# One list of all engines' work from the first instruction to the end of the second stage, with due times worked back from the products

## The chip, the cores and the metric

The kernel runs on one core of a Trainium2 chip. The metric is the device time of one launch in microseconds (us). In this text PE is TensorE, DVE is VectorE, ACT is ScalarE, POOL is GpSimd and SP is SyncE, whose queue issues the DMAs.

## The reference

Three stages follow each other on 4 sequences of 768 tokens (3072 tokens in all). All arithmetic on the chip is float32; the weights arrive as 64-bit floats.

```
# 1 retention, 8 heads of 64, per sequence b and head h
state = gamma[h] * state + outer(k[t], v[t])
x[t]  = q[t] @ state / 8
# 2 expert layer, 512 -> 2048 -> 512
h = x @ w_in
g = where(h >= 1, h, where(h <= -1, 0, (h + 1)**2 / 4))
x2 = g @ w_out
# 3 expert layer, 512 -> 1024 -> 512
h2 = x2 @ w2_in
u  = h2 * softmax(h2)
out = ((u - mean) / sqrt(var + 1e-6) * g_ln) @ w2_out
```

## The kernel before

**Precision.** A product takes each operand as a rounded part and a remainder (hi, lo) and adds hi·hi, lo·hi and hi·lo, so each product of the layers is three matmuls. Each 128x512 matmul streams 512 columns.

**Weights.** A weight piece (128 rows of 512 numbers) comes as 64-bit words. `conv_w` (L259 to L283) makes float32 words of them: ACT L264 and L267, DVE L265, L268, L269, L270; then the hi part on ACT (L275) and the lo part on DVE (L276). w_in and w_out have 16 pieces each. For pieces from `KEEP` = 4 on, `conv_w` also stores the float32 words to DRAM (`wim`, `wom`, L281).

**Blocks.** The tokens are 6 blocks of 512; four attention units of 128 tokens fill one block, so there are 24 units. A unit is scores (16 small matmuls), a mask on DVE (`sm`), the part that comes from the running state (8 matmuls, or 16 quarter-size ones from unit 12 on), the part within the unit (16), and the new state (16). A sequence has 6 units; its first unit reads no state and its last makes none.

**First stretch, the direct form.** Blocks 0 and 1 go through the first expert layer directly, in 32 slots of one weight piece each: `moe_h` (L529, 12 matmuls), activation on ACT and DVE (L535 to L537, L243, L244), `moe_out` (L557, 12 matmuls). `weights_slot` loads and converts pieces some slots ahead. Units 0 to 15 run beside it, in `attention`. `prep` makes the left operands of the second form from the weights of a pair of pieces: it takes the float32 words (from DRAM through `back`, or for the first `KEEP` pieces as hi + lo, L595), forms four sums (L602), splits them (L243, L244 on 128x1024) and stores seven left operands per pair to DRAM (`wia`, `woa`, L611 and L613): three copies of 256 KB and two stores of 512 KB. The order of this whole stretch is made by the framework's scheduler from the order of the code and its priorities.

**Second stretch, the seven-product form.** Blocks 2 and 3, then 4 and 5, go through the same layer with seven products in place of eight (a Strassen scheme). A first gemm has 8 x 7 products of six matmuls (L947), a second gemm 7 x 8 (L1095). Their left operands are read back from DRAM by `stream` (L700), 256 KB each, four to a buffer. Units 16 to 23 run inside the first of the four gemms (L747 scores, L785, L791, L797). The order comes from the class `Plan`: each task has an engine, a cost, predecessors, a due time given by hand and buffers that it takes; `run` lists them in simulated time, earliest possible first, PE in the order of the code. All five engines then run in that order (`in_row`).

**Third stage.** Loops in the order of the code; PE L1285, L1326 and L1337.

**Buffers.** Most tiles of 4 KB per partition come from one pool "w" with `NWS` = 27 buffers. A unit's q and k tile `qk` has 2 buffers; the result of a unit from 16 on is written into that tile and stored from there (`xrd`, L814), so that the tile comes free when that store has landed.

Of the kernel before, what the change touches and what calls it, by code (L numbers as in the profile page):

```python
# [38 lines left out]
KEEP = 4  # L39
KVACT = 8  # L40
PREP = 12
NWS, NOPS = 27, 6
# [25 lines left out]
class Slot:  # L68


    def __init__(self, pool):
        self.pool, self.users, self.left, self.end = pool, [], 0, None
# [6 lines left out]
class Task:  # L79
    def __init__(self, eng, cost, fn, deps, due, take):  # L80
        self.eng, self.cost, self.fn, self.due, self.take = eng, cost, fn, due, take
        self.deps = [d for d in deps if d is not None]
        self.start = self.end = self.gate = None


class Plan:
# [3 lines left out]
    WAIT = 0.15  # L90

    def __init__(self, caps):
        self.tasks, self.caps, self.clock, self.products, self.lead = [], caps, 0.0, [], 1

    def add(self, eng, cost, fn, deps=(), due=0.0, take=()):
        t = Task(eng, cost, fn, deps, due, take)
        if eng != "PE" and len(self.products) >= self.lead:
            t.gate = self.products[-self.lead]
        self.tasks.append(t)
        return t  # L100

    def ahead(self, lead):

        self.lead = lead

    def pe(self, cost, fn, deps=(), take=()):
        t = self.add("PE", cost, fn, deps, self.clock, take)
# [5 lines left out]
    def run(self):  # L113
        todo, after, slots = {}, {}, {p: [] for p in self.caps}
        ready = {e: [] for e in ("PE", "DVE", "ACT", "POOL", "SP")}
        order = [t for t in self.tasks if t.eng == "PE"][::-1]
        for t in self.tasks:
            before = t.deps + ([t.gate] if t.gate else [])
            todo[t] = len(before)
            for d in before:  # L120
                after.setdefault(d, []).append(t)
            if not before:
                ready[t.eng].append(t)
        uses = {}
        for t in self.tasks:
            for s in t.take:
                s.left = len(s.users)
                for u in s.users:
                    uses.setdefault(u, []).append(s)
        free, dma, left = dict.fromkeys(ready, 0.0), 0.0, len(self.tasks)  # L130

        def can(t):

            at = max([free[t.eng]] + [d.end + Plan.WAIT for d in t.deps] + ([t.gate.start] if t.gate else []))
            for p in {s.pool for s in t.take}:
                n = sum(s.pool == p for s in t.take)
                ends = sorted(9e9 if s.end is None else s.end for s in slots[p])
                over = len(ends) + n - self.caps[p]
                if over > 0:
                    at = max(at, ends[over - 1] + Plan.WAIT)  # L140
            return at

        while left:
            best = None
            for e, ts in ready.items():
                if e == "PE":
                    ts = [t for t in ts if t is order[-1]]
                for t in ts:
                    at = can(t)
                    k = (at if at > free[e] else free[e], t.due)  # L150
                    if at < 9e8 and (best is None or k < best[0]):
                        best = k, t
            if best is None:
                raise RuntimeError(f"the plan is stuck: {[(t.eng, t.due, [s.pool for s in t.take]) for ts in ready.values() for t in ts if t.eng != 'PE' or t is order[-1]]}")
            (at, _), t = best
            ready[t.eng].remove(t)
            if t.eng == "PE":
                order.pop()
            t.start = at
            free[t.eng] = at + (0.34 if t.eng == "SP" else t.cost)  # L160
            if t.eng == "SP":
                dma = max(dma, at + 1.6) + t.cost
                t.end = dma + 0.6
            else:
                t.end = at + t.cost
            for s in t.take:
                slots[s.pool] = [x for x in slots[s.pool] if x.end is None or x.end + Plan.WAIT > at] + [s]
            for s in uses.get(t, ()):
                s.left -= 1
                if not s.left:  # L170
                    s.end = max(u.end for u in s.users)
            t.fn()
            left -= 1
            for u in after.get(t, ()):
                todo[u] -= 1
                if not todo[u]:
                    ready[u.eng].append(u)
        return max(t.end for t in self.tasks if t.eng == "PE")
# [3 lines left out]
def kernel(  # L182
# [64 lines left out]
    wi, wo = {}, {}  # L247
    state = {}

    def load_w(src, pool=wp):  # L250
        raw = pool.tile([128, 512, 2], U32, tag="w", name="w_raw")
        state["last_w"] = nc.sync.dma_start(raw.rearrange("p a t -> p (a t)"), src.bitcast(U32))
        return raw
# [3 lines left out]

    def conv_w(raw, scale=None, w=None, keep=None):
        lw, hw = raw[:, :, 0], raw[:, :, 1]  # L259
        m = cv.tile([128, 512], F32, tag="wm", name="wm", bufs=3)  # L260
        p = cv.tile([128, 512], F32, tag="wp", name="wp", bufs=2)
        mu, mi = m.bitcast(U32), m.bitcast(I32)

        sc.activation(m, hw.bitcast(F32), AF.Abs)  # L264
        ve.tensor_scalar(m, m, W_MIN, W_MAX, op0=ALU.max, op1=ALU.min)  # L265

        sc.activation(p, lw, AF.Copy, bias=2.0, scale=2.0 ** -51)  # L267
        ve.tensor_scalar(mu, mu, 3, None, op0=ALU.logical_shift_left)  # L268
        ve.scalar_tensor_tensor(mu, hw, 0x80000000, mu, op0=ALU.bitwise_and, op1=ALU.bitwise_xor)  # L269
        ve.tensor_tensor(out=mi, in0=mi, in1=p.bitcast(I32), op=ALU.add)  # L270
        if w is None:
            w = wp.tile([128, 2, 512], F32R, tag="w", name="w")
        hi, lo = w[:, 0, :], w[:, 1, :]
        if scale is None:
            sc.activation(hi, m, AF.Copy)  # L275
            ve.tensor_tensor(out=lo, in0=m, in1=fl(hi), op=ALU.subtract)  # L276
        else:
            sc.activation(hi, m, AF.Copy, scale=scale)
            ve.scalar_tensor_tensor(lo, m, scale, fl(hi), op0=ALU.mult, op1=ALU.subtract)
        if keep is not None:  # L280
            nc.sync.dma_start(keep, m)  # L281
        return w

# [18 lines left out]
    def attention(u, env):  # L302
        b, c = divmod(u, NCH)
        first, last = c == 0, c == NCH - 1
        blk, cb = divmod(u, CPB)
        attp = env["attp"]
        if blk == 0:
            def banks(*names):
                return [ps_acc.tile([128, 512], F32, tag="acc", name=n) for n in names]
        else:  # L310
            both = []

            def banks(*names):

                if not both:
                    both.append(ps_a.tile([128, 2, 512], F32, tag="pa", name="pa"))
                return [both[0][:, n] for n in range(len(names))]
        early, quad = u < NWP, u >= QUAD

        def tile_of(name, *shape):  # L320
            if early:
                return wp.tile([128, 2, *shape], F32, tag="w", name=name)
            return attp.tile([128, 2, *shape], F32, tag=name, name=name, bufs=2)

        qk, kv = tile_of("qk", NPAIR, C), tile_of("kv", H, D)
        with (ExitStack() if early else tc.issue_after(state["last_w"].ins)):
            if not quad:
                nc.sync.dma_start(qk, qk_t[b, c])
            else:
                load_swapped(qk, qk_t[b, c])  # L330
            nc.sync.dma_start(kv, kv_t[b, c])
        yield
        yield
        if u == QUAD:

            env["gdec"] = gdec2
            with tc.issue_after(state["last_w"].ins):
                load_swapped(qdec, xtab_d)
                load_swapped(gdec2, gdec_d)
            gp.tensor_tensor(out=qdec, in0=qdec, in1=gdec2.to_broadcast([128, NPAIR, C]), op=ALU.mult)  # L340
            swap = wp.tile([128, 2, 2, C], F32, tag="w", name="swap")
            for r in range(2):
                sc.activation(swap[:, r], dmat[:, r, 2:], AF.Copy)
            for r in range(2):
                sc.activation(dmat[:, r, 2:], swap[:, 1 - r], AF.Copy)
        qp = [t.rearrange("a (p c) -> a p c", p=NPAIR) for t in banks("qp0", "qp1")]
# [1072 lines left out]
```

## Time and profile before

| | us |
|---|---|
| median of 3 runs | 913.42 (911.47 to 914.26) |
| the profiled execution | 916.41 |
| its span, first to last instruction | 914.7 |
| PE busy / weight loads busy | 877.1 / 715.1 |
| DVE busy / ACT busy | 751.1 / 507.0 |
| mean granted PE clock | 0.981 of full speed |

A busy PE is one with a matmul in flight, by modelled ends; it says nothing of the rate. The rate is read from the distance between starts. A granted clock of 1.0 is the higher of two levels (2.4 GHz), 0.5 the lower (1.2 GHz).

### The profile page before, as it was taken

The numbers are of one execution on the slowest core, as the hardware profiler recorded it, in microseconds if no ns is written. First come the engines' busy times: TensorE is split into PE (matmuls) and PEld (weight loads), VectorE is DVE, ScalarE is ACT, GpSimd is POOL, SyncE is SP. The second block draws the span as 40 slices with busy tenths as digits, with TensorE's granted clock in tenths as the row PEclk, the third lists the DMA queues.
The fourth block names the chain that finished last, engine by engine and source line by source line (L and its number), as shares of the span: only waits on it lengthen the run. The fifth ranks groups of instructions, "written<-read, shape, count | busy, mean of one in ns | idle before, by whom it ended". The sixth has DMA issues, their size and how long they took to land. (4 is left out here: it accounts for less than half of the span.)

```text
span 914.7 us, 13934 instructions
## 1 busy us (share of the span) xinstructions
PE 877.1 (96%) x4824; PEld 715.1 (78%) x4824; DVE 751.1 (82%) x1592; ACT 507.0 (55%) x995; POOL 60.0 (7%) x56
## 2 busy tenths in 40 slices
PE   7899899969999999999989999999999999999998
PEld 7777688848887777788868778888888888888886
DVE  4998898888956767697988989796988888888885
ACT  2767875867756779764537877542333333233322
POOL 3100000000000101000111110017000000000000
PEclk8999999979999999899999999999999999999999
DMA  9849968999997998796668887887110110100000
GB/s 337 343 162 339 344 233 271 383 346 369 338 296 239 313 286 289 240 381 231 224 184 294 317 316 231 294 298 253 58 69 25 45 49 28 65 24 24 24 24 34
DMA packets 108567, 197.08 MB, mean 215 GB/s; under 512 B 10193, under 2 KB 49489, under 8 KB 107729
## 3 DMA queue, kind: packets, MB, share of 16 engines
q1 hardware_dynamic: 108496, 196.20, 62.4%
q8 instruction: 38, 0.62, 0.3%
q14 instruction: 33, 0.26, 0.1%
HBM read 135.34 MB, written 60.82 MB: 214 GB/s over the span
## 5 line engine op out<-in xcount | busy, mean ns | idle before, releaser
L1095 PE MATMUL yp<-go,left 128*128 128x512 f32 x672 | 153.9, 390 | 1.9 <-DVE go L1061 1.7
L1095 PEld LDWEIGHTS yp<-go,left 128*128 128x128 f32 x672 | 125.9, 188 | 29.2 <-DVE go L1061 3.1
L947 PE MATMUL hp<-xoh,left 128*128 128x512 f32 x448 | 126.1, 404 | 5.5 <-DVE cs L1144 2.3
L947 PEld LDWEIGHTS hp<-xoh,left 128*128 128x128 f32 x448 | 83.5, 192 | 28.9 <-DVE gl L996 3.2
L1057 ACT ACTIVATE go<-g 128x512 fp32r<-128x512 f32 x112 | 69.3, 629 | 58.7 <-PE yp L1095 28.3
L1285 PE MATMUL h2p<-w,x2h 128*128 128x512 f32 x384 | 97.1, 395 | 0.0
L1337 PE MATMUL op<-w,lh 128*128 128x512 f32 x384 | 91.4, 390 | 0.2 <-ACT lh L243 0.2
L1061 DVE TENSOR_TENSOR go<-g,go 128x512 fp32r<-128x512 f32 x112 | 77.1, 702 | 11.9 <-ACT go L1057 11.0
L1337 PEld LDWEIGHTS op<-w,lh 128*128 128x128 f32 x384 | 71.9, 188 | 15.4 <-ACT lh L243 0.5
L1285 PEld LDWEIGHTS h2p<-w,x2h 128*128 128x128 f32 x384 | 70.5, 188 | 13.9 <-ACT x2h L243 0.3
L529 PE MATMUL hp<-xh,w 128*128 128x512 f32 x256 | 68.7, 408 | 4.3 <-DVE cs L537 3.4
L557 PE MATMUL acc<-gh,w 128*128 128x512 f32 x256 | 68.4, 395 | 2.1 <-ACT xs L563 1.5
L947 PE MATMUL hp<-xol,left 128*128 128x512 f32 x224 | 69.9, 394 | 0.0
L1295 ACT ACTIVATE e<-h2p,st 128x512 f32<-128x512 f32 x48 | 32.6, 685 | 60.8 <-DVE st L1293 45.6
L243 ACT ACTIVATE x2h<-x2r 128x512 fp32r<-128x512 f32 x24 | 15.2, 632 | 84.8 <-PE h2p L1285 64.1
L529 PEld LDWEIGHTS hp<-xh,w 128*128 128x128 f32 x256 | 49.0, 195 | 16.9 <-DVE cs L537 4.6
L557 PEld LDWEIGHTS acc<-gh,w 128*128 128x128 f32 x256 | 47.3, 188 | 13.9 <-ACT xs L563 1.9
L1285 PE MATMUL h2p<-w,x2l 128*128 128x512 f32 x192 | 51.4, 390 | 0.0
L922 DVE SCALAR_TENSOR_TENSOR g<-cs,g 128x512 f32<-128x512 f32 x48 | 37.1, 777 | 17.3 <-ACT cs L921 17.3
L947 PEld LDWEIGHTS hp<-xol,left 128*128 128x128 f32 x224 | 42.7, 191 | 9.4
L641 DVE TENSOR_TENSOR g<-g 128x512 f32<-128x512 f32 x64 | 48.8, 768 | 0.0
L1337 PE MATMUL op<-w,ll 128*128 128x512 f32 x192 | 47.7, 390 | 0.0
(156 smaller groups left out, 1582.2 us busy)
## 6 DMA issues: line engine op xcount, KB each, us to landing
left<-wia SPq DMA_DIRECT2D x112, 256.0 KB, 5.0
left<-woa SPq DMA_DIRECT2D x112, 256.0 KB, 4.3
kv<-in_kv_t_dram SPq DMA_DIRECT2D x24, 512.0 KB, 6.7
w_raw<-in_w_in_dram SPq DMA_DIRECT2D x24, 512.0 KB, 6.9
w_raw<-in_w_out_dram SPq DMA_DIRECT2D x24, 512.0 KB, 6.6
qk<-in_qk_t_dram SPq DMA_DIRECT2D x12, 512.0 KB, 8.1
wia<-w SPq DMA_DIRECT2D x24, 256.0 KB, 5.5
woa<-w SPq DMA_DIRECT2D x24, 256.0 KB, 5.7
```

The source lines that it names most:

```text
L243: sc.activation(hi, src, AF.Copy)
L529: pe.matmul(hp, l[:, k * 128:(k + 1) * 128], r[:, k, :], start=(n == 0), stop=(n == 3 * KD - 1))
L557: pe.matmul(acc[d][:, :BLK], l[:, d * 128:(d + 1) * 128], r, start=(first and m == 1), stop=(last and m == 3))
L641: ve.tensor_tensor(out=b[o], in0=b[l], in1=b[r], op=ALU.subtract)
L922: x = DVE(U512, lambda: ve.scalar_tensor_tensor(put(), c["t"], 1.0, get_h(), op0=ALU.min, op1=ALU.max), (q,), due + 1.5)
L947: pe.matmul(e[bank], w[i][:, k * 128:(k + 1) * 128], x[j][:, k], start=(first and m == 0), stop=(last and m == 3 * KH - 1), skip_group_che ...
L1057: sc.activation(t[:, 0], quarters_g(n)[q], AF.Copy)
L1061: ve.tensor_tensor(out=lo, in0=quarters_g(n)[q], in1=fl(hi), op=ALU.subtract)
L1095: pe.matmul(e["banks"][j], w[:, s, j * 128:(j + 1) * 128], g[t], start=(n == 0 and c == 0), stop=(n == NP - 1 and c == 2))
L1285: pe.matmul(hps[n], l[:, k, :], w2i[k, n][:, part], start=(m == 0), stop=(m == 3 * KD - 1))
L1295: sc.activation(e[:, n, :], hps[n], AF.Exp, bias=st[:, 2:3], accum_out=st[:, 3 + n:4 + n])
L1337: pe.matmul(op, l[:, f, :], w2o[f][:, part], start=(n == 0), stop=(n == 3 * NF2 - 1))
```

## The change

Everything from the first instruction to the end of the second stretch now goes through `Plan`: attention units 0 to 15, the direct form, the weight conversion and `prep` become tasks like the others, and `attention`, `weights_slot`, `conv_w`, `back` and `att_slot` go.

- `Plan.run` makes up to four lists and keeps the one whose simulated end is earliest. `late` works each task's latest start back from the fixed places of the PE tasks, through its successors and through the buffers of the list before; among the tasks that could start within 0.12 us the one that must be done first is taken. In the first stretch PE tasks may overtake each other within six places (`WINDOW`).
- The simulated costs have a tail for each engine, a turn between kinds of matmul, a limit of eight DMAs in flight, and DVE and POOL sharing a port. The three DVE steps at the start of a conversion are three tasks, where the second stretch had one.
- The float32 words of a pair of pieces (from `KEEP` = 6 on) stay in a "w" buffer until their sums are formed; they no longer go to DRAM and back. Pairs 0 to 2 form them as hi + lo, in slots 13, 16 and 19.
- The left operands lie in DRAM in the order in which PE takes them, two to a tile `lefts` with rows of 4 KB; `stream` reads two with one load of 512 KB. The sums are split in two halves, and `prep` makes seven stores of 256 KB.
- A unit's result from 16 on goes into the tile `qn` (now 2 buffers), so that `qk` comes free after the scores and the scaling of q. In units 0 to 11 the new state's matmuls come before those within the unit.
- `NWS` is 26, and the decay of k for units 4 to 7 moves from POOL to ACT (`KVACT` 8 to 4). Loads of units 16 to 23 may start 20 products ahead, where it was 10.

```diff
-KEEP = 4
-KVACT = 8
-PREP = 12
-NWS, NOPS = 27, 6
+KEEP = 6
+KVACT = 4
+PREPS = (13, 16, 19)
+NQN = 2
+CAHEAD = 25.0
+NWS, NOPS = 26, 6
...
+    TAIL = {"PE": 0.13, "DVE": 0.14, "ACT": 0.2, "POOL": 0.06, "SP": 0.06}
+    QUEUE = 2.5
+    CHANNELS = 8
+    TURN = 0.13
+    WINDOW = 6
...
+        for t in reversed(order):
+            if t.eng == "PE":
+                t.latest = t.goal = t.v
+                continue
+            ends = [u.latest for u in after.get(t, ())]
+            if t.due is not None:
+                ends.append(t.due)
+            t.goal = min(ends) if ends else t.at + 10.0
+            t.latest = t.goal - self.long(t)
...
-                    ts = [t for t in ts if t is order[-1]]
+                    ts = [t for t in ts if t is order[-1] or t.v < self.loose and t in order[-Plan.WINDOW:]]
...
+                _, at, t = min(((t.goal, at, t) for at, t in found if at < first + 0.12), key=lambda k: k[0])
...
-    wia = [dpool.tile([128, 7, 2, 256], F32, tag=f"wia{n}", name=f"wia{n}") for n in range(NP)]
-    woa = [dpool.tile([128, 7, 2, 256], F32, tag=f"woa{n}", name=f"woa{n}") for n in range(NP)]
-    wim = {f: dpool.tile([128, 512], F32, tag=f"wim{f}", name=f"wim{f}") for f in range(KEEP, NF)}
-    wom = {f: dpool.tile([128, 512], F32, tag=f"wom{f}", name=f"wom{f}") for f in range(KEEP, NF)}
+    lefts = [dpool.tile([128, 2, 2, 256], F32, tag=f"left{n}", name=f"left{n}") for n in range(7 * NP)]
...
-        if keep is not None:
-            nc.sync.dma_start(keep, m)
+                if not j:
+                    pair["t"] = wtile("wm", F32, 2, 512)
+                c["m"] = pair["t"][:, j]
...
-        hi = wp.tile([128, 4, 256], F32R, tag="w", name="wsh")
-        lo = wp.tile([128, 4, 256], F32R, tag="w", name="wsl")
-        split(sm, hi, lo)
+        for k, keys in enumerate(((5, 6), (7, 3))):
+            def hi(k):
+                c["hl", k] = wtile("wsh", F32R, 2, 2, 256)
+                sc.activation(c["hl", k][:, :, 0], c["s"][:, 2 * k:2 * k + 2], AF.Copy)
...
-            nc.sync.dma_start(fl(tile_["t"][:, q]), src)
+                nc.sync.dma_start(fl(tile_["t"][:, q:q + 2]), lefts[p // 2])
+            t = DMA(512, f, [left_ready[i] for i in (p, p + 1)], 0, () if q else (slot,), ahead=16.0, run=4)
...
+                return (e["qk"][:, 0] if first else e["qn"])[:, 2 * g:2 * g + 2] if away else env["x"][blk][g][:, :, tk]
...
-        hook(max(t0 - 10, 0), lambda u=u: att_load(u, plan.clock))
+        hook(max(t0 - 20, 0), lambda u=u: att_load(u, plan.clock))
```

## Rows read from the trace of the kernel before

**Rows 1.** Stretches: us, then each engine's busy us (instructions), clock, DMA share, GB/s.

```profile
0.00:29.10 29.10, 23.68 (x256) 21.16 (x256) 16.96 (x32) 11.47 (x24) 8.23 (x13) 0.88 0.96 352
29.10:271.20 242.10, 226.54 (x1416) 182.16 (x1417) 209.40 (x374) 172.02 (x342) 3.68 (x3) 0.96 0.89 308
271.20:393.20 122.00, 115.64 (x818) 90.96 (x819) 84.01 (x135) 94.17 (x211) 11.02 (x8) 0.96 0.85 278
393.20:468.10 74.90, 73.03 (x319) 59.29 (x318) 68.87 (x103) 40.14 (x63) 3.00 (x2) 1.00 0.74 257
468.10:555.00 86.90, 82.64 (x355) 65.88 (x355) 75.94 (x112) 64.58 (x109) 14.83 (x10) 1.00 0.84 288
555.00:627.10 72.10, 72.10 (x320) 59.69 (x319) 63.60 (x97) 35.90 (x59) 11.90 (x11) 1.00 0.84 280
627.10:913.00 285.90, 283.48 (x1345) 235.93 (x1343) 232.32 (x745) 88.76 (x190) 7.30 (x10) 1.00 0.13 48
```

**Rows 2.** PE in order of time (start, us, line, shape, count): work at full rate.

```profile
555.01 72.24 PE L1095 MATMUL yp<-go,left 128*128 128x512 f32 x318
...
135.60 1.16 PE L351 MATMUL pa<-qk 64*128 64x128 f32 x16
136.69 1.19 PE L557 MATMUL acc<-gl,w 128*128 128x512 f32 x4
137.72 1.99 PE L529 MATMUL hp<-xh,w 128*128 128x512 f32 x8
...
144.31 1.05 PE L424 MATMUL pa<-qn,state 128*128 128x128 f32 x8
...
146.78 0.97 PE L529 MATMUL hp<-xh,w 128*128 128x512 f32 x3
...
224.80 0.67 PE L392 MATMUL pa<-qn,state 64*64 64x128 f32 x16
...
226.89 1.65 PE L557 MATMUL acc<-gh,w 128*128 128x512 f32 x6
```

**Rows 3.** PE in order of time: stops, their length and cause in brackets.

```profile
107.05 3.33 PE L529 MATMUL hp<-xh,w 128*128 128x512 f32 x8 [1.82 <-DVE cs L537]
...
196.27 2.08 PE L351 MATMUL pa<-qk 64*128 64x128 f32 x16 [5.54 <-DVE state L412]
...
473.46 1.20 PE L947 MATMUL hp<-xoh,left 128*128 128x512 f32 x4 [2.32 <-DVE cs L1144]
```

**Rows 4.** DVE in order of time: its first step on data, two back to back.

```profile
7.60 0.71 DVE L472 TENSOR_TENSOR dmat<-dmat,vdec 128x512 f32<-128x512 f32 x1 [6.58 <-DMA dmat<-in_xtab_dram]
...
124.67 0.69 DVE L244 TENSOR_TENSOR gl<-cs,gh 128x512 fp32r<-128x512 f32 x1
125.28 0.42 DVE L268 TENSOR_SCALAR wm<-wm 128x512 uint32<-128x512 uint32 x1
```

**Rows 5.** Windows of 20 us in the first stretch, columns as in rows 1.

```profile
40.00:60.00 20.00, 19.52 (x119) 15.18 (x120) 19.93 (x38) 14.84 (x25) 1.11 (x1) 1.00 0.53 175
...
260.00:280.00 20.00, 19.99 (x99) 16.06 (x98) 5.28 (x8) 8.82 (x15) 0.00 (x0) 1.00 0.90 287
```

**Rows 6.** Waits up to 627 us: who for whom, us in all, times, longest.

```profile
PE pa L351 <- DVE state L412: 5.5, 1, 5.5
PE pa L747 <- DMA qk<-in_qk_t_dram: 5.1, 4, 1.9
```

**Rows 7.** Waits of SP's queue to 271 us: stores' longest sum, loads' longest.

```profile
SPq L611 <- DVE w L276: 27.5, 11, 5.1
...
SPq L252 <- DMA kv<-in_kv_t_dram: 2.6, 3, 1.0
```

**Rows 8.** DMA issues: count, KB each, median us to landing.

```profile
left<-wia SPq DMA_DIRECT2D x112, 256.0 KB, 5.0
...
w_raw<-in_w_in_dram SPq DMA_DIRECT2D x24, 512.0 KB, 6.9
...
wim<-wm SPq DMA_DIRECT2D x12, 256.0 KB, 5.7
```

More of the change, by code (lines that the diff above doesn't have):

```diff
@@ L172, in run @@
-            t.fn()
+                    insort(ends[s.pool], max(u.end for u in s.users))
+                    freed[s.pool].append(s)
+            out.append(t)
             left -= 1
@@ L300, in load_swapped, with temp @@
                               src[(slice(64 - 64 * h, 128 - 64 * h), *ax, slice(n, 2 * n))])
-    def attention(u, env):
-        b, c = divmod(u, NCH)
[L304 to L318, printed above, removed]
+    def temp(tag):
+        return moe.tile([128, BLK], F32, tag=tag, name=tag, bufs=GB)
@@ L350, in attention @@
                     r = slice(64 * o, 64 * o + 64)
[L351 to L355 removed]
+                    pe.matmul(e["qp"][o][:, p, :], e["qk"][r, 1, p, :], e["qk"][r, 0, p, :], start=True, stop=True)
+        t = e["scores"] = plan.pe(0.9, f, (e["lq"],), e["pa_slots"], mode="rows")
@@ L421, in attention @@
[L421 to L430 removed]
+            else:
@@ new lines, in state @@
+        def state():
+            _, sp = views()
+            kv = e["kv"]
+            for p in range(NPAIR):
+                for r in range(2):
+                    h = 2 * p + (r ^ (p // 2 if quad else 0))
+                    pe.matmul(sp[64 * r:64 * r + 64, p, :], kv[:, 0, h, :], kv[:, 1, h, :],
+                              start=True, stop=True, skip_group_check=True)
+        ta = tb = None
+        if not first:
+            ta = plan.pe(0.4 if quad else 0.89, cross, [e["sm_task"][r] for r in range(2 if quad else 1)] + [e["qn_task"], st_task[0]], mode="quarters" if quad else "words")
+            e["qn_slot"].used(ta)
+            st_task[1] = ta
@@ new lines, in sums @@
+        def sums():
+            return plan.pe(0.42, state, [e["scores"], e["sm_task"][1], e["lk"], ta] + e["kd"], mode="halves")
+        if not last and not quad:
+            tb = sums()
+        t = plan.pe(0.82, within, [e["sm_task"][r] for r in (1, 0)] + [e["lk"], ta], mode="halves")
+        if not last and quad:
+            tb = sums()
+        for x in (t, tb):
+            if x:
+                e["kv_slot"].used(x)
+        for r in range(2):
+            e["sm_slot"][r].used(t)
+        v = t.vend
@@ L621, with p @@
-    SEQ1 = (1, 5, 6, 2, 3, 7, 4)
-    LEFT = {1: 0, 2: 1, 4: 2, 5: 3, 6: 4, 7: 5, 3: 6}
+            acc["slots"] = [Slot("acc") for _ in range(KD)]
+        def p(part):
+            w = wo[f]["w"]
+            if first and not part:
+                for d in range(KD):
+                    acc[d] = ps_acc.tile([128, 512], F32, tag="acc", name="acc")
+            three = ((0, g["h"]), (1, g["h"]), (0, g["l"]))
+            seq = [(d, n) for n in range(3) for d in range(KD)] if not last else [(d, n) for d in range(KD) for n in range(3)]
+            for d, n in seq[6 * part:6 * part + 6]:
+                l, r = three[n]
+                pe.matmul(acc[d], cut(w, l, d), r, start=(first and n == 0), stop=(last and n == 2))
```

1225 lines of the change are left out of this document (627 added, 598 removed).

## The prediction

> **What bounds the kernel now.** I read the stretches first. The reader should cut the span at 29.1, 271.2, 393.2, 468.1, 555.0 and 627.1 us: A is units 0 to 3, B the direct form, C to F the four gemms, G the third stage [rows 1]. In F and G PE is busy all but 2.4 of 358 us, and the code of G hardly changes. So whatever the change is worth lies before 627.1 us.
>
> How much can lie there is read from the rate, not from the busy share. In F 318 matmuls take 72.24 us, 0.227 each; six make a product of 1.36 [rows 2]. A unit's scores take 1.09, and the four matmuls behind them 1.03 where four take 0.91, so a turn costs 0.1: 1.3 with both turns. The rest of a unit takes 2.47, or 2.6 with turns; from unit 12 on 2.09, or 2.2. A full unit is thus 3.9, later 3.5 less a little: I use 3.4. A first unit lacks the state part (1.0, later 0.6), a last one the new state (0.55).
>
> Then each stretch at full rate:
> A: 4 x 3.9 - 1.0, and 5.4 of start and warming up: 20.0 of 29.1, so 9.1 are lost.
> B: 768 matmuls are 174.3; units 4 to 11 give 31.2 - 1.0 - 1.1 = 29.1, units 12 to 15 give 13.0: 216.4 of 242.1, 25.7 lost.
> C: 59 products are 80.4; eight units 27.2 - 1.7 = 25.5: 105.9 of 122.0, 16.1 lost.
> D: 53 products 72.2 of 74.9, 2.7 lost. E: 59 products 80.4 of 86.9, 6.5 lost. F: nothing.
> Together 60 us. That is the most that the change can return, and the floor is a span of 914.7 - 60 = 855.
>
> PE is without a matmul for only 33.5 of these (busy sum before 627.1 us: 593.6). Most of the others are the lower clock after a stop: behind the 1.82 us stop at 107.05 eight matmuls last 3.33 us, where eight last 1.99 in the same view, 1.3 more; the granted clock of A to C is 0.88, 0.96 and 0.96, of D to F 1.00 [rows 1 to 3]. The Trainium skill (Trainium Kernel Development and Optimization, Performance Expectations) calls matmul busy time a bad measure and the busy share of weight loads a good one. By matmul busy time 33.5 us could be won; by weight loads, with F's 82.8% as full, A to F need 479.1 / 0.828 = 578.7 of 627.1 us, 48.4 to be won. My count of 60 comes from the rows above and is nearer to the second.
>
> What ends the stops? In B DVE: the longest is a state copy of DVE for which PE stands 5.5 us; in C it is the loads of q and k, 5.1 us in four stops [rows 3, 6]. DVE is the busiest engine beside PE in A and B: 226.4 us of 271.2. It is packed at 99.6% from 40 to 60 us, and idle for 14.7 of the 20 us from 260 on, while the first gemm already has its operands [rows 1, 5]. So B is limited by DVE at its beginning and not at its end.
>
> **The change part by part.**
>
> One list for A and B. It removes no work of PE. On DVE it adds four adds of hi and lo for the pair that `KEEP` 6 brings in (0.61 each by the distance of two steps, 2.4) and splits sixteen long steps into halves (some 0.06 each, 1.0) [rows 4]. DVE's need is then 226.4 + 3.4 = 230, from 7.6 us on, when its first table has landed [rows 4]. If DVE were kept full at the share that it has in F, 63.60 of 72.10 or 88%, A and B would end at 7.6 + 230 / 0.88 = 269: 2 us won. If it reached 97% and 10 us of `prep` moved behind A and B, it would take 234, and PE's own 236.4 decides: 35 won. That move is open: the left operands of the second gemm aren't read before C's end, and DVE has 38 us idle in C [rows 1]. The rows lie on both sides (88% where PE is full and nothing presses, 99.6% where work is heaped up), and an isolated step counts 0.08 too long (0.69 by its bar, 0.61 by the distance), so a tight list needs less than 230. I take 93% and 5 us moved: 7.6 + 225 / 0.93 = 249.5, 22 won, with 2 to 35 as bounds. Bringing the new state forward and sharing weight conversion with the waits in A are part of these 22, not beside them.
>
> Units 16 to 23 in C. A q and k tile now comes free after scores and scaling, where it waited for a store to land; with loads allowed 20 products ahead instead of 10. The four stops of 5.1 us go. What is late next is ACT, 94 us busy of a stretch that would be 106 long, 89%. C's other 11 us are the lower clock behind those stops and small waits; half of it goes with the stops. I take 10 won, with 5 (the waits alone) and 16 (all) as bounds, so C is 112 us. The 5 us of DVE work moved in there raise it to 89 of 112, which is less than F's share.
>
> D and E. The same code under a list that knows that a DVE step depending on the one before it starts later. E's largest stop, 2.32 us, waits for the last sum of the gemm before [rows 3]. I take 1 in D and 2 in E; bounds 0 and 9.2 together.
>
> Costed at nothing: the float32 words not stored and loaded (24 stores and 24 loads of 256 KB, 12.6 MB of the 85 that A and B move by their rates), left operands in 112 loads of 512 KB instead of 224 of 256 KB, and seven stores for five per pair [rows 1, 8]. No PE wait on a left operand or a weight is among the waits before; the largest on a DMA is that for q and k [rows 6]. That is because the loads run ahead by several products; if that cover went, each late weight would cost up to its 6.9 us to landing [rows 8]. SP's queue stands for 27.5 us behind stores of left operands that wait for DVE [rows 7]. A store still waits there, but loads are what must not be late, and the list puts a store where it expects its data. The moved decays, three units of eight steps, are some 6 to 8 us of ACT, which has 70 us idle in B [rows 1].
>
> Sum: 22 + 10 + 3 = 35. From the profiled 916.4 that is 881; it stands 3.0 over the median of the runs shown, 913.4, from which it is 878. I take 879.
>
> **The rivals.**
>
> DVE is the bound and stays it. If the list keeps DVE no denser than F does, A and B return 2 us and C to E 13: 898. For it speaks that DVE's need of 230 us is more than the 228.8 us between its start at 7.6 and PE's floor of 236.4 [rows 4]. Against it: the 14.7 idle us at B's end, and work that may move into C.
>
> Nearly all is returned: 35 in A and B, 16 in C, half of D and E, 55: 858. It wants DVE at 97% for 230 us. No row shows such a share over more than a window of 20 us.
>
> Weights come late for want of buffers, and it gets slower. The words of each pair now hold a "w" buffer from the first conversion to the sums, the weights of the first six pieces hold theirs until slots 13, 16 and 19, and there is one buffer less. When the pool is full, a weight load stands at the head of SP's queue until a store has landed (5.7 us), and all loads behind it stand too [rows 8]. The place is slots 12 to 27, where ten pieces arrive. If PE stands 3.5 us for each, the 35 are used up; with 4.5 each it is +10: 923. The Trainium skill (TensorE: Matmul & The Clock Gate, the table of specifications) states that the queues of VectorE, ScalarE and GpSimd are strictly first in, first out; by it a late load would also hold back every DVE step listed behind its conversion; no row here shows that by itself. Against this rival: today the line that loads weights, L252, waits 2.6 us in all at its worst, 1.0 at the longest [rows 7], and the list counts buffers.
>
> Nothing changes: what B and C return is lost again where ACT or SP become the limit. No row points there; C's ACT has 12 us to spare.
>
> **How the numbers follow.** The forecast (866 to 890) has a chance of 0.58; DVE stays the bound (890 to 908) 0.19; nearly all returned (853 to 866) 0.07; no change 0.04; slower 0.12. The time is that of the forecast, 879. The range is 862 to 905: the upper part of the floor's case and nearly all of DVE's, leaving out slower, no change and the rest, some 0.2. A measurement of this kernel tells 0.3% (2.7 us) from no change. Faster 0.84, same 0.04, slower 0.12.
>
> **What would show it.** Right: the first L947 product starts near 250 us instead of 271.2, DVE is above 90% from 20 to 240 us and no longer idle after 260, no PE wait of the scores of units 16 to 23 for q and k, the next gemm 112 us later, granted clock of B and C at 0.98 or above, G still 286 us. DVE's rival: DVE packed as now and C starting after 262. The slower one: SP's weight loads waiting for stores or PE waiting for converted weights in slots 12 to 27. Wrong altogether would be a B that is as long as before with DVE less busy, for then an order, not an amount, set its length.

## The result, and the profile after

The changed kernel takes 891.91 us (median of four runs, 891.42 to 894.60) against 913.84 (four runs, 911.47 to 915.47): a ratio of 0.977, 95% interval 0.974 to 0.980, so 21 to 22 us faster. The prediction was 879 us and 862 to 905: faster, as forecast, by some 60% of the amount. The profiled execution took 891.42 us, its span 889.7.

By stretch, in us, with the same boundaries as in [rows 1]. The full-rate column is the working of the prediction.

| | A | B | C | D | E | F | G | span |
|---|---|---|---|---|---|---|---|---|
| full rate | 20.0 | 216.4 | 105.9 | 72.2 | 80.4 | 72.1 | | |
| before | 29.1 | 242.1 | 122.0 | 74.9 | 86.9 | 72.1 | 287.6 | 914.7 |
| after | 32.1 | 227.9 | 107.8 | 72.8 | 81.2 | 76.5 | 291.4 | 889.7 |
| difference | +3.0 | -14.2 | -14.2 | -2.1 | -5.7 | +4.4 | +3.8 | -25.0 |

C, D and E now run within 2 us of full rate each. B keeps 11.5 us, A 12.1. F and G, which the prediction left alone, lost 8.2 between them.

The stretches of the changed kernel (columns as in rows 1):

```profile
0.00:32.10 32.10, 20.89 (x256) 18.75 (x256) 17.12 (x32) 12.30 (x27) 7.54 (x12) 0.84 0.91 344
32.10:260.00 227.90, 221.34 (x1416) 176.14 (x1417) 208.24 (x394) 178.82 (x383) 1.49 (x1) 1.00 0.78 271
260.00:367.80 107.80, 107.80 (x819) 86.16 (x818) 76.37 (x124) 88.52 (x200) 11.68 (x8) 1.00 0.89 288
...
440.60:521.80 81.20, 80.86 (x356) 66.31 (x355) 63.57 (x92) 59.17 (x97) 12.83 (x10) 1.00 0.79 277
521.80:598.30 76.50, 73.48 (x320) 59.28 (x319) 76.50 (x119) 42.22 (x72) 14.35 (x12) 1.00 0.91 318
```

The granted clock of B and C went from 0.96 to 1.00; that of A fell from 0.88 to 0.84. PE has no idle time in C, where it had 6.4 us. In F the relation is turned round: DVE is busy for all of it and PE for 73.5 of 76.5 us, where PE had been full and DVE at 88%. DVE also has more to do there: 24 of its conversion steps for the third stage's weights (tile `wm`) now lie in F, where before none did; E had 40 of them and has 17. The `wm` steps in F, before and after (us, DVE's and ACT's busy us, then clock, DMA share, GB/s):

```profile
555.00:627.10 72.10, 0.00 (x0) 0.00 (x0) 1.00 0.84 280
521.80:598.30 76.50, 14.03 (x24) 5.43 (x9) 1.00 0.91 318
```

DVE and PE in B, in windows of 20 us, beside [rows 5]:

```profile
40.00:60.00 20.00, 18.97 (x146) 14.52 (x146) 19.34 (x38) 17.50 (x41) 0.00 (x0) 1.00 0.58 205
...
240.00:260.00 20.00, 20.00 (x90) 16.55 (x89) 7.74 (x11) 11.14 (x20) 0.00 (x0) 1.00 0.86 266
```

The ten windows from 40 to 240 us hold 192.7 us of DVE work, 96%; the last one of B holds 7.7 of 20. DVE still has an idle tail while PE runs full.

PE's waits up to 620 us (waiter, releaser, us, times, longest; the third stage starts at 598.3), beside [rows 6]:

```profile
PE pa L533 <- DMA qk<-in_qk_t_dram: 4.4, 1, 4.4
PE h2p L1360 <- DVE st L1377: 2.8, 1, 2.8
PE pa L590 <- DVE sm L558: 2.7, 3, 1.4
PE yp L1111 <- DVE go L1079: 2.4, 3, 1.2
```

The wait for a state copy (5.5) and the four for q and k in C (5.1) are gone. The largest is new and stands at the very start. The second is new too and lies in G, where PE waits for DVE's first row statistics; it is most of G's 3.8 us. SP's queue in order of time shows why the first is there: the first q and k load, which was issued at 0.80 us (first line, of before), now goes out behind the tables (the lines under it).

```profile
0.80 0.39 SPq L328 DMA_DIRECT2D qk<-in_qk_t_dram  x1
...
0.80 0.39 SPq L456 DMA_DIRECT2D vdec<-in_vdec_dram  x1
1.25 2.49 SPq L459 DMA_DIRECT2D dmat<-in_xtab_dram  x4
...
4.42 0.43 SPq L506 DMA_DIRECT2D qk<-in_qk_t_dram  x1
```

Its first scores then start at 9.39 us, where they had started at 5.37:

```profile
5.37 1.16 PE L351 MATMUL qp<-qk 64*128 64x128 f32 x16
...
9.39 2.08 PE L533 MATMUL pa<-qk 64*128 64x128 f32 x16 [4.39 <-DMA qk<-in_qk_t_dram]
```

DMA: loads of left operands, and SP's waits up to 260 us, beside [rows 7, 8]:

```profile
left<-left SPq DMA_DIRECT2D x112, 512.0 KB, 5.3
```

```profile
SPq L824 <- DVE w L428: 33.7, 11, 6.8
...
SPq L382 <- DMA kv<-in_kv_t_dram: 3.5, 4, 0.9
```

As predicted, stores still wait in SP's queue for DVE (33.7 us in the largest sum, 27.5 before), and the weight loads of L382 for little (3.5 us in the largest sum, 0.9 at the longest). Bytes fell from 197.1 to 184.5 MB, packets from 108567 to 71701.

Last, the end of F, PE in order of time and under it DVE and POOL (the last line is of the trace of before):

```profile
521.76 66.58 PE L1111 MATMUL yp<-go,left 128*128 128x512 f32 x292
588.94 1.65 PE L1111 MATMUL yp<-go,left 128*128 128x512 f32 x6 [0.60 <-DMA x2q<-x2p]
591.23 1.66 PE L1111 MATMUL yp<-go,left 128*128 128x512 f32 x6 [0.64 <-DVE go L1079]
593.51 1.66 PE L1111 MATMUL yp<-go,left 128*128 128x512 f32 x6 [0.62 <-DVE go L1079]
596.34 2.12 PE L1111 MATMUL yp<-go,left 128*128 128x512 f32 x8 [1.16 <-DVE go L1079]
```

```profile
585.02 0.68 DVE L1079 TENSOR_TENSOR go<-g,go 128x512 fp32r<-128x512 f32 x1
588.23 4.68 POOL L1341 TENSOR_TENSOR x2r<-x2r,x2q 128x256 f32<-128x256 f32 x4 [0.49 <-DMA x2q<-x2p]
...
588.81 1.22 DVE L886 TENSOR_TENSOR g<-g 128x512 f32<-128x512 f32 x1
589.95 1.23 DVE L1079 TENSOR_TENSOR go<-g,go 128x512 fp32r<-128x512 f32 x1
591.10 1.21 DVE L886 TENSOR_TENSOR g<-g 128x512 f32<-128x512 f32 x1
592.23 1.22 DVE L1079 TENSOR_TENSOR go<-g,go 128x512 fp32r<-128x512 f32 x1
...
594.56 10.60 POOL L1341 TENSOR_TENSOR x2r<-x2r,x2q 128x256 f32<-128x256 f32 x12
```

```profile
618.34 5.01 POOL L1266 TENSOR_TENSOR x2r<-x2r,x2q 128x256 f32<-128x256 f32 x5 [6.31 <-DMA x2q<-x2p]
```

PE runs over 66 us without a stop and then stops before each of the last products. What it waits for is a DVE step of 512 columns, 0.68 us long at 585.02. (The row of the first stop names a load, but the DVE step of 588.21, 0.68 us long, ends 0.05 us before that product starts.) From 588.81 on such steps last 1.22 and start 1.14 apart, while POOL adds the halves of token block 0 for the third stage. A product needs two of them, 2.28 us, and the starts of the products behind 588.94 lie 2.29, 2.28 and 2.83 apart where a product itself takes 1.36. The adds stand in no list: the third stage is issued in code order. In the trace of before they began at 618.34 us, 8.8 before the end of F; here they begin 10.1 before it, and this time with seven of the last products' DVE steps still to come (three then, the last of them done 4.4 us before F's end). DVE, full since the start of F, has nothing in hand when they come.

### The profile page after: what moved, and what is told of

The parts are those of the page before. It is cut to its first block, busy times and chain, and to the rows that moved or that the text cites. A ratio compares the mean times of both kernels' runs of the same rounds, so it can differ in the third digit from the quotient of the medians.

```text
span 889.7 us, 13728 instructions
## 1 busy us (share of the span) xinstructions
PE 861.6 (97%) x4824; PEld 703.3 (79%) x4824; DVE 744.9 (84%) x1612; ACT 512.9 (58%) x1035; POOL 62.2 (7%) x53
## 4 chain that ended last, share of the span: by engine, by line
PE 65%; DVE 19%; DMA 8%; ACT 6%; issue 2%; SPq 1%; DVEq 0%; ACTq 0%
PE hp L965 16%; PE h2p L1360 15%; PE op L1412 15%; PE yp L1111 8%; DVE go L1079 5%; DMA w_raw<-in_w_in_dram 4%; PE acc L785 4%; DVE g L886 3%; PE tp L1401 2%; PE hp L746 2%; DMA x2p<-cs 1%; DVE w L428 1%; DVE wm L409 1%; PE pa L533 1%; PE pa L601 1%
## 5 line engine op out<-in xcount | busy, mean ns | idle before, releaser
L965 PE MATMUL hp<-xoh,left 128*128 128x512 f32 x448 | 121.8, 394 | 0.0
L1079 DVE TENSOR_TENSOR go<-g,go 128x512 fp32r<-128x512 f32 x112 | 80.8, 732 | 2.8 <-ACT go L1075 2.7
L785 PE MATMUL acc<-gh,w 128*128 128x512 f32 x256 | 71.4, 400 | 0.0
L727 ACT ACTIVATE cs<-cs 128x512 f32<-128x512 f32 x96 | 59.8, 627 | 1.4
L746 PEld LDWEIGHTS hp<-xh,w 128*128 128x128 f32 x256 | 46.7, 188 | 13.0 <-DVE cs L728 1.9
L1415 ACT ACTIVATE o<-op,st 128x512 f32<-128x512 f32 x24 | 16.5, 687 | 58.3 <-PE op L1412 48.2
L1367 DVE TENSOR_REDUCE st<-h2p 128x1 f32<-128x512 f32 x48 | 32.1, 689 | 20.3 <-PE h2p L1360 20.3
```

What stands on the lines that cost most here:

```text
L727: q = ACT(A512, lambda: sc.activation(c["t"], c["t"], AF.Square), (r,), due + 0.5)
L746: pe.matmul(c["h"], cut(w, part, k), r[:, k, :], start=(n == 0), stop=(n == 3 * KD - 1))
L785: pe.matmul(acc[d], cut(w, l, d), r, start=(first and n == 0), stop=(last and n == 2))
L965: pe.matmul(e[bank], w[i][:, k * 128:(k + 1) * 128], x[j][:, k], start=(first and m == 0), stop=(last and m == 3 * KH - 1), skip_group_che ...
L1079: ve.tensor_tensor(out=lo, in0=quarters_g(n)[q], in1=fl(hi), op=ALU.subtract)
L1367: ve.tensor_reduce(st[:, n:n + 1], hps[n], axis=AX.X, op=ALU.max)
```

## The experiments

Times are set against the kernel before on the same chip; the changed kernel stands at 0.977. Where a run is said to be so many us over or under the changed kernel, that is the difference of the two ratios times 913.84 us; with the intervals of the two it is known to 3 or 4 us. Stretches are of one profiled execution each. One measure of care: x_order, x_vadd, x_hold and x_hold10 have the changed kernel's instructions in the same order on every engine through A and B, and these two together take 263.8, 261.8, 261.5 and 261.1 us where the changed kernel's profiled execution took 260.0. A difference of 3 us in one stretch of one execution is therefore not an effect by itself.

### The order of the blocks in the third stage (x_order)

```diff
+        TURNS = (2, 3, 0, 1, 4, 5)
-            nc.sync.dma_start(t, x2d[blk])
+            b = TURNS[blk]
+            nc.sync.dma_start(t, x2d[b])
-            if blk < 2:
+            if b < 2:
-            nc.sync.dma_start(out[t * 128:(t + 1) * 128, :], o)
+            row = TURNS[t // TPB] * BLK + t % TPB * 128
+            nc.sync.dma_start(out[row:row + 128, :], o)
```

> The third stage takes the blocks in the order 2, 3, 0, 1, 4, 5, so that no POOL add (block 0 and 1 alone have them) falls into the end of the last gemm. Theory: POOL's adds make DVE's steps there last 1.2 us instead of 0.6, and PE waits for them; then the last gemm loses its stops (2.4 us) and the third stage is back at 287 to 288 us from 291: 885 to 887. Rival: the operands are listed too close to their products (6 us), whatever POOL does; then both stay, 890 to 892.

Measured: 0.9666 (0.9644 to 0.9688), 885.94 us, 9.3 us under the changed kernel. F and G together take 358.8 us, where the changed kernel has 367.9 and the kernel before 359.7. POOL's adds now come in the third stage:

```profile
638.36 6.06 POOL L1343 TENSOR_TENSOR x2r<-x2r,x2q 128x256 f32<-128x256 f32 x8 [42.95 <-DMA x2q<-x2p]
```

This gives back the whole loss of F and G. It does not show by which path: the new order also lets third-stage products of blocks 2 and 3 fill PE's gaps from 492.9 us on, so that the adds' absence and the filling act together. DVE's 24 conversion steps lie in F here too; what they would cost without the filling this run can't tell.

### The adds on DVE (x_vadd)

```diff
-                gp.tensor_tensor(out=part, in0=part, in1=q[n][:, :, j * 128:(j + 1) * 128], op=ALU.add)
+                ve.tensor_tensor(out=part, in0=part, in1=q[n][:, :, j * 128:(j + 1) * 128], op=ALU.add)
```

> The adds of the halves of blocks 0 and 1 run on DVE instead of POOL; the order of the blocks is that of the changed kernel. Theory: POOL beside DVE is what makes DVE's steps double at the end of the last gemm; then the last gemm and the third stage together return from 367.9 to 359 to 362 us. Rival: the gain of the other order of blocks came from products of the third stage that fill PE's gaps in the last gemm; then these two stay at 366 to 369.

Measured: 0.9772 (0.9744 to 0.9799), no difference. F and G take 371.1 us. DVE in order of time, with POOL's one remaining pair:

```profile
588.56 2.97 POOL L1155 TENSOR_TENSOR gh<-gh,cs 128x512 f32<-128x512 f32 x2 [9.13 <-DVE cs L1153]
588.93 1.47 DVE L886 TENSOR_TENSOR g<-g 128x512 f32<-128x512 f32 x1
...
592.60 2.42 DVE L1341 TENSOR_TENSOR x2r<-x2r,x2q 128x256 f32<-128x256 f32 x7
```

The doubling is where POOL works and nowhere else: DVE's steps stay 0.6 us apart except in the 3 us of that pair. But DVE now makes the adds itself, among the last operands, and PE then waits 5.8 us for DVE's first row statistics of the third stage (2.8 in the changed kernel). In this run the adds cost as much on DVE as they had on POOL.

### The second gemm's operands 12 us ahead (x_lead)

```diff
-            ... rd[o] + [wr[k] for k in {o, l, r}], due, ahead=7.0)
+            ... rd[o] + [wr[k] for k in {o, l, r}], due, ahead=13.0)
-            h = ACT(A512, a, (wr[q],), due, (s_,), ahead=6.0)
+            h = ACT(A512, a, (wr[q],), due, (s_,), ahead=12.0)
```

> The right operands of the second gemms may be made 12 us (sums 13) ahead of their latest start instead of 6 and 7. Theory of POOL: it takes hold only while DVE still has operands to make; if they are made earlier, the last gemm has no stops and the two last stretches take 360 to 363 us instead of 367.9. Rival: only six operand buffers exist, so DVE can't run further ahead whatever the permission; 366 to 369.

Measured: 0.9756 (0.9728 to 0.9784), F 77.7 and G 291.5: no effect. DVE is busy for 77.7 of F's 77.8 us there, so an earlier permission to start doesn't bring the operands earlier. Whether the six operand buffers, which the rival named, would hold them back as well, the run doesn't show.

### The first load ahead of the tables (x_start)

```diff
+    att_load(0, -60.0)
+    before_ = len(plan.tasks)
     tables()
+    for t_ in plan.tasks[before_:]:
+        if t_.eng == "SP":
+            t_.forced = [cells[0]["lq"]]
-    for u in range(3):
+    for u in range(1, 3):
```

> Unit 0's load of q and k goes ahead of the tables. Theory: the start lost 3 us because the list puts five table loads and kv in front of it; then the first scores start near 5.4 us instead of 9.4, the first product of the direct form at 28 to 29 instead of 32.1, and all that follows is 3 to 4 us earlier: 888. Rival: from 40 us on the amount of DVE's work sets the pace, and an earlier start of PE is eaten up there: the seven-product form still starts at 259 to 260, 891 to 892.

Measured: 0.9711 (0.9690 to 0.9732), 5.2 us under the changed kernel by the ratios; the profiled span is 2.1 shorter. A takes 29.6 us, C starts at 258.2. SP's queue and PE at the start:

```profile
1.25 0.42 SPq L506 DMA_DIRECT2D qk<-in_qk_t_dram  x1
```

```profile
6.12 1.16 PE L533 MATMUL pa<-qk 64*128 64x128 f32 x16 [0.59 <-DMA qk<-in_qk_t_dram]
```

So A's new 3 us are the place of this one load, 4.42 us instead of 0.80, and 1.8 of A's 2.5 us are still there where C starts. The list, which ranks loads by when their users must start, had put it behind tables that the scores don't read.

### One more DVE step per slot (x_dve)

```diff
+        def more():
+            ve.tensor_tensor(out=cc["t"], in0=cc["t"], in1=fl(g["h"]), op=ALU.subtract)
+        b2 = DVE(U512, more, (b,))
```

> Each slot of the direct form has one DVE step of 512 more (32 steps, 19 us of DVE; its result isn't used). Theory: DVE's amount sets the pace of the direct form from 40 to 230 us; its end moves by 8 to 19 us (what doesn't fit into DVE's 12 idle us at the stretch's end). Rival: the order of the tasks and the waits between engines set it, and DVE has room; it moves by under 4 us.

Measured: 0.9872 (0.9836 to 0.9909), 9.5 us over the changed kernel by the ratios; the profiled span is 13.7 longer. C starts at 272.0, 12.0 later; later stretches hardly change. The added steps are 32 by 0.6, 19 us; B's row:

```profile
33.60:272.00 238.40, 224.87 (x1417) 176.91 (x1417) 227.94 (x425) 180.65 (x383) 1.26 (x1) 0.99 0.73 255
```

DVE is 20 us busier and B 10.5 longer, with PE full for 224.9 of 238.4. DVE's amount sets the pace of B also in the changed kernel; about 7 of the 19 us fitted into its idle tail. (The list was made anew with the added steps, which also hold two buffers a little longer; how much of the 12 us that is stays open.)

### The result written to the q and k tile again (x_hold), and loads 10 ahead (x_hold10)

```diff
-                return (e["qk"][:, 0] if first else e["qn"])[:, 2 * g:2 * g + 2] if away else ...
+                return e["qk"][:, 0, 2 * g:2 * g + 2] if away else ...
-                e["qk_slot" if first else "qn_slot"].used(z)
+                e["qk_slot"].used(z)
```

x_hold10 has, besides, the second edit of C undone:

```diff
-        hook(max(t0 - 20, 0), lambda u=u: att_load(u, plan.clock))
+        hook(max(t0 - 10, 0), lambda u=u: att_load(u, plan.clock))
```

> Units 16 to 23 write their result into the q and k tile again, so that it comes free only when the store has landed. Theory: this is what made the gemm beside them 14 us shorter; it grows by 5 to 14 us, 897 to 906. Rival: the permission to load 20 products ahead instead of 10 did it; it grows by less than 2 us, 892 to 894.

> Both at once for units 16 to 23: the result stays in the q and k tile until its store has landed, and loads may start 10 products ahead instead of 20. Theory after the run with the first half alone (the gemm grew by 2.6 us only): the two cover each other, and without both the loads are late again as in the kernel before; the gemm beside the units grows from 107.8 to 115 to 122 us and PE waits 3 to 6 us for q and k. Rival: the gemm got shorter by the order of ACT's and DVE's steps and by less DMA traffic; it stays under 112 us.

Measured: x_hold 0.9773 (0.9753 to 0.9794) with C at 110.4 and 0.7 us of PE's waits for q and k in two stops, x_hold10 0.9778 (0.9746 to 0.9809) with C at 108.5. The instructions of the two stand in the same order on every engine, so x_hold10 is a second run of x_hold: allowing the loads 20 products ahead changes nothing here. What holds them back in both is the tile: in C, x_hold10's loads go out 0.1 to 1.2 us after the store before them has landed. C's row in x_hold10:

```profile
261.10:369.60 108.50, 108.50 (x819) 86.72 (x819) 77.71 (x124) 88.43 (x200) 11.19 (x8) 1.00 0.88 287
```

PE is busy without a gap although the tile again waits for its store. Early release is worth 0.7 to 2.6 us of C's 14.2, and the 20 products nothing beside it.

The release does bring the loads forward: from unit 18 on the last part of a unit's q and k lands 1 to 15 us before its scores start in the changed kernel, and between 1.4 us before and 0.8 after in x_hold10. That this is still in time goes with results that come sooner. From a unit's first score to the end of its last result step (ACT L811, then L666) it takes 12.2 to 16.0 us in the trace of before and 10.1 to 13.1 in x_hold10, so that store and reload start earlier. Which step of the list made the results sooner no run shows.

### Ranking by hand-given due times (x_due)

```diff
+            t.rank = t.at if t.due is None else t.due
-                _, at, t = min(((t.goal, at, t) for at, t in found if at < first + 0.12), key=lambda k: k[0])
+                _, at, t = min(((t.rank, at, t) for at, t in found if at < first + 0.12), key=lambda k: k[0])
```

> The lists are ranked by the due times given by hand, or by a task's place among the products where none is given, and no longer by the latest times worked back; loads, buffers and everything else are as in the changed kernel. If the worked-back due times are what made the third stretch 14 us shorter (122.1 to 107.8), as neither the early release of the q and k tile nor the loads 20 products ahead was, that stretch comes out at 112 to 120 here and the kernel some 8 to 20 us over the changed one, at 0.986 to 0.999 of the time before. The rival, that the list's gaps between dependent steps, the smaller DMA traffic and the emptier third-stretch queues made it, wants 107 to 109 for the third stretch and less than 4 us in all (0.973 to 0.981).

Measured: 1.0154 (1.0137 to 1.0171), 927.99 us: 35 us over the changed kernel and slower than before. But not in C, which takes 109.1 us: the theory's own number fails, and its rival's holds for that stretch. The loss is A +17.6, B +9.0, D +8.2, E +5.0; F and G are 4.4 shorter. In A, PE makes one stop of 18.27 us; PE's row, and under it the DVE steps it waits behind:

```profile
44.62 2.04 PE L591 MATMUL pa<-qn,state 128*128 128x128 f32 x8 [18.27 <-DVE state L705]
```

```profile
24.23 0.42 DVE L401 TENSOR_SCALAR wm<-wm 128x512 f32<-128x512 f32 x1
...
41.21 0.68 DVE L559 TENSOR_TENSOR sm<-pa,dmat 128x512 f32<-128x512 f32 x1
41.81 0.68 DVE L410 CUSTOM_DVE_ANT_0 wm<-wm,wp 128x1024 uint16<-128x1024 uint16 x1
42.41 0.41 DVE L705 TENSOR_TENSOR state<-pa,state 64x256 f32<-64x256 f32 x1
```

PE had its last matmul before this stop at 26.4 us, so the state's sums were there; the first step that reads them ran at 42.41 (the second, at 44.05, ends the stop), behind 18 us of DVE steps without a gap, nearly all of them weight conversion. DVE is busy all the time and with the wrong things, and its busy share can't tell this from B's good order; PE's stop can. The Trainium skill (TensorE: Matmul & The Clock Gate, the table of specifications) states that VectorE's queue is strictly first in, first out; these rows agree with it.

### Words through DRAM again (x_words)

```diff
-        raw_s, m_s, p_s = Slot("w"), pair["slot"] if pair else Slot("wm"), Slot("wp")
+        raw_s, m_s, p_s = Slot("w"), Slot("wm"), Slot("wp")
+            z = DMA(256, lambda: nc.sync.dma_start(d_, c["m"]), (t4,))
+            ...
+                nc.sync.dma_start(pair["t"][:, j], d_)
```

> The float32 words of the pairs from piece 6 on go to DRAM and come back, as before (20 stores and 20 loads of 256 KB more). Theory, as predicted: hidden, within 2 us of 892. Rival: SP's queue and the DMA engines are full enough in the direct form that weights come late; 897 to 907.

Measured: 0.9816 (0.9785 to 0.9847), 4.4 us over the changed kernel, with intervals that overlap; B 233.3 us, 5.4 longer than in the changed kernel and 3 to 4 longer than in x_order and x_vadd, with DVE's busy time as it was (209.1). PE's longest wait, and the new stores in SP's queue:

```profile
PE h2p L1363 <- ACT x2h L322: 4.3, 1, 4.3
```

```profile
SPq L444 <- DVE wm L406: 13.7, 10, 3.1
```

The words' transfers seem to cost a few us, with no wait of PE on any of them; PE's 4.3 us at the start of the third stage stand in F and G, which together are 3.8 longer. That SP is held up by its new stores (13.7 us in ten waits) could be the cause in B, but the list came out in another order too, and this run doesn't show which of them it is.

### Left operands in two loads of 256 KB (x_left256)

```diff
-                nc.sync.dma_start(fl(tile_["t"][:, q:q + 2]), lefts[p // 2])
+                for i in range(2):
+                    nc.sync.dma_start(fl(tile_["t"][:, q + i]), lefts[p // 2][:, i])
```

> Each pair of left operands is read by two loads of 256 KB with rows of 2 KB instead of one of 512 KB with rows of 4 KB. The prediction costed this part of the change at nothing: within 2 us of the changed kernel, 0.975 to 0.979 of the time before. The rival: 112 more issues on SP and twice the packets cost 3 to 8 us in the four gemms, seen as PE waits on left operands, and explain a part of what the third to fifth stretches gained.

Measured: 0.9844 (0.9827 to 0.9861), 898.95 us, 6.9 over the changed kernel. The rival's number, but not its sign: no PE wait is on a left operand. 4.0 of the span's 6.8 us are in E, at one stop and the lower clock behind it (0.90 granted from 442.7 to 460 us, 1.00 in the changed kernel's first 17 us of E):

```profile
448.17 1.15 PE L966 MATMUL hp<-xoh,left 128*128 128x512 f32 x4 [2.57 <-ACT gh L992]
```

The listing came out otherwise for all engines, since its simulated DMA costs changed. This run can't tell the loads' own price from that.

### Four buffers fewer (x_nws)

```diff
-NWS, NOPS = 26, 6
+NWS, NOPS = 22, 6
```

> 22 buffers in the pool for weights and words instead of 26. The prediction's slower rival held that words kept in these buffers leave too few for the weights. If buffers are scarce, four fewer cost 5 to 30 us, most of it in the direct form (227.9 us in the changed kernel), with stops of PE or loads of weights waiting for buffers. If there is slack, the direct form stays within 3 us and the whole within 0.974 to 0.981 of the time before.

Measured: 1.0279 (1.0249 to 1.0310), 939.05 us: 47 us over the changed kernel, more than either theory gave. B takes 255.0, C 114.7, E 89.7, G 301.0 (the third stage draws on the same pool). Two windows of B, PE's longest stop there, and SP's queue:

```profile
60.00:80.00 20.00, 11.89 (x76) 9.76 (x77) 14.70 (x27) 7.73 (x16) 0.00 (x0) 0.74 0.22 81
80.00:100.00 20.00, 19.05 (x147) 14.83 (x146) 11.13 (x21) 8.83 (x17) 0.00 (x0) 1.00 0.21 66
```

```profile
66.73 2.08 PE L533 MATMUL pa<-qk 64*128 64x128 f32 x16 [7.54 <-issue]
```

```profile
62.38 17.05 SPq L824 DMA_DIRECT2D left<-w  x6
79.47 0.92 SPq L382 DMA_DIRECT2D w_raw<-in_w_in_dram  x2
```

```profile
SPq L824 <- DVE w L428: 54.6, 17, 19.3
```

For 17 us SP's queue stands at six stores of left operands, and no weight load goes out; DMA is at 0.22, and in the 40 us DVE has 25.8 of work. This is the slower rival's picture, with four buffers less. The longest single wait at that line is 19.3 us here (last line), with 26 buffers 6.8. For PE's stop itself the trace names no releaser ("issue").

### Both repairs together (x_best)

The edits of x_order and x_start.

> The third stage takes the blocks in the order 2, 3, 0, 1, 4, 5 and the first unit's q and k load goes ahead of the tables, both together. By their single results (8.8 and 4.1 us under the changed kernel, on the ratio to the time before) the sum would be 0.961 of the time before; if the start's gain is lost again behind the direct form, 0.965 to 0.967, the same as the block order alone. Theory: 0.959 to 0.964, about 880 us.

Measured: 0.9639 (0.9624 to 0.9653), 880.58 us: faster than both kernels, 33 us under the one before and 12 under the changed one. A takes 29.9, C starts at 257.5, F and G together 358.9. Two DVE steps where POOL's adds had been:

```profile
590.59 0.68 DVE L886 TENSOR_TENSOR g<-g 128x512 f32<-128x512 f32 x1
591.19 0.68 DVE L1079 TENSOR_TENSOR go<-g,go 128x512 fp32r<-128x512 f32 x1
```

The two gains add up to within 3 us (9.3 and 5.2 make 14.5; 11.8 came).

## Why the prediction was right, and where its sizes were off

**Direction and place.** What the change is worth came before the third stage, from stops of PE and the lower clock behind them, as the first step said. B, C, D and E gave 36.2 us of the 60 counted as lost, and none of them ended below its counted full rate.

**A and B, 22 forecast, 11.2 measured: mis-sized.** DVE's need was right: 225.4 us of work before C, where 230 less 5 moved was the figure. Its density was not. 225.4 us in the 252.4 from 7.6 us on are 89%, not 93%. In the middle it is better than assumed, 96%; what is missing is the start (15.6 of the 24.5 us of A behind 7.6) and the tail (7.7 of the last 20). x_dve shows that more DVE work still makes B longer. The rival "DVE is the bound and stays it" is thus nearer than the prediction had it: 891.9 lies in its band (890 to 908), just outside the forecast's (866 to 890). Its terms were not met, though: C starts at 260.0, not after 262, and C to E returned 22 us instead of 13; what brings the time into its band is the loss in F and G. That C to E returned 9 us more than the 13 counted made up for most of the 11 missing in A and B, and that is luck, since C's gain came without the cause named for it. The late first load, which no step of the prediction looked at, cost A 2.5 of this, as x_start shows (1.8 at C's start).

**C, 10 forecast, 14.2 measured: inside the bounds, and the cause it named isn't needed.** The four stops for q and k went, and with them the lower clock, as said. But the step named the early release and the 20 products, and undoing both costs 0.7 to 2.6 us: under the new list results come sooner, and the loads are just in time without either. Neither the ranking (x_due, 109.1), nor the words (108.0), nor the 512-KB loads (107.9) carries the rest alone. What all these kernels share is that each load's earliest start is worked back from its users, and that the simulated costs count tails and turns; undoing either was not tried, and the cause of some 12 us of C stays open.

**D and E, 3 forecast, 7.8 measured.** Inside the bounds given. x_due makes D and E 13.2 us longer: the worked-back ranking is needed for them.

**F and G, 0 forecast, 8.2 lost: the step that failed.** "The code of G hardly changes" was true and not enough. When F's last operands are made later, or G's first adds earlier, two things meet that had all but missed each other, DVE's last operands and POOL's adds. Nor was F left as it was: with the 24 conversion steps that the list moved into it, DVE has 76.5 us of work there instead of the 63.6 that the prediction read, and no slack to make up for slower steps. That these steps had a part in the loss is argued from the rows; no run moved them back. x_order returns 9.1 us. How much of that is the adds' absence and how much the products that fill F stays open: x_vadd took POOL out and lost as much on DVE.

**Costed at nothing.** The words are worth some 4 us (x_words), at the edge of what the runs tell. For the left operands 6.9 us stand against nothing, though not as a transfer's price.

**The slower rival.** Buffers decide, but 26 are enough. The edge is near: with 22 the kernel is 2.8% slower than before, with SP's queue behind stores as that rival described.

**Sum.** Measured terms: -11.2 in A and B, -14.2 in C, -7.8 in D and E, +8.2 in F and G, together -25.0 of the profiled 916.4. With F and G as before and the first load in its place, 891.4 - 8.2 - 2.5 = 880.7 would be left, which is what x_best takes (880.58) and near the forecast; but in that sum the 9 us too many from C to E stand against the 8 still missing in A and B.

## What to carry to other kernels

A list of instructions improves what it lists and can harm what it doesn't: check the seam to the code behind it, and the first ten DMAs, as closely as the middle. Tell a good order from a bad one by PE's stops, since the engine that feeds it is as busy in either. When an edit changes a list, compare the lists before giving a stretch's gain to the edit: here one edit named as a cause had left the order of every engine unchanged. A run that undoes one part tells what the part is worth beside the others, not what it would do alone: the early release brought loads forward by up to 15 us and was worth next to nothing.

## What the runs showed of the hardware that was not expected

- A DVE step on two 128x512 float32 operands takes 0.68 us by its bar and 0.60 by the distance of two steps; while POOL adds two tensors of 128x256 it takes 1.21 to 1.23 by its bar and 1.14 by the distance, and beside an add of 128x512 up to 1.77 and 1.70 (593.38 us, L886). POOL's adds of 128x256 suffer too: 0.76 us each in x_order's third stage (8 in 6.06, with one such DVE step beside them), 1.17 at the end of F of the changed kernel (4 in 4.68). The Trainium skill (SBUF — State Buffer, Who interferes with whom) states that a DVE instruction with two SBUF inputs contends with a GpSimd instruction that reads SBUF, over a shared pair of ports that only one of them holds at a time. The rows agree in kind: a step of one and an add of the other start at nearly the same distance, 1.14 and 1.17. They are 0.2 short of the 1.36 that the two take one after the other (0.60 and 0.76). The prediction named POOL's adds nowhere.
- The same order of instructions took 260.0 to 263.8 us for A and B in five profiled executions (the changed kernel, x_hold10, x_hold, x_vadd, x_order).
